# Down weights of a one-token decode block in three loads of 21, 6 and 1 rows in place of five

## The chip, the cores and the metric

The kernel runs on one core of one Trainium2 chip. Its time is the device time of one execution in microseconds. The engines that matter here are TensorE (PE in the profile; its weight loads are PEld), VectorE (DVE), ScalarE (ACT) and SyncE (SP), whose queue issues the loads of weights and caches. The loads themselves are carried by 16 DMA engines.

## The reference

One token passes through a transformer block: layer norm, grouped-query attention over a cache of 65,536 positions, a residual, a second layer norm and a gated feed-forward network. All inputs are bfloat16.

```python
x: [1, 1, 1024]; k_cache, v_cache: [1, 4, 65536, 128]; wq: [1024, 4096]; wo: [4096, 1024]
w_gate, w_up: [1024, 3584]; w_down: [3584, 1024]

def _A_ref(x, k_cache, v_cache, wq, wo):      # 32 query heads on 4 key/value heads
    q = (x @ wq) in heads
    p = softmax(q @ k^T * 128 ** -0.5)
    return (p @ v) joined @ wo

def _B_ref(x, w_gate, w_up, w_down):
    return (gelu(x @ w_gate) * (x @ w_up)) @ w_down

h = x + _A_ref(layernorm(x), ...)
h2 = h + _B_ref(layernorm(h), ...)
```

The caches are 134 MB, the five weight matrices 39 MB; every byte of them is read once.

## The kernel before

All of it goes through one buffer in SBUF, `ring`, of five units of 16,384 bfloat16 columns on 128 partitions. `load` (L167 issues the transfer on SP's queue) places each load at the next free unit. SP issues the loads in the order of the program and waits, before each, until the matmuls that read the old contents of those columns are done, and until the old contents have landed. Transfers are carried out in the order of their issue.

The attention part takes keys and values of four heads through the ring. Then come the output projection (`wo`, two loads), the residual and the second layer norm, and the feed-forward part, in which this change lies. The vector of the token is the stationary operand (32 columns, of which one is used), and the weights stream past it. Four matmuls at a time work side by side, each on 32 columns of the array. The gate matrix `wg` comes in one load of 7168 KB (ring columns 16384 to 45055), the up matrix `wu` in two loads of 3584 KB (columns from 49152 on). Their products are copied out of PSUM, turned by TensorE (`turned`, L156), and joined to the activation `act_bf`, which `padded` writes to `actz`.

The down matrix has 3584 rows; partition p holds 28 of them, one after the other, so "28 rows" here means 28 rows for each of the 128 partitions, 256 KB a row. The loop at the end loads them in groups. `at[0] = 0` and the offset `c0 * D` put all groups side by side at the ring's columns 0 to 28671: a row takes 1024 columns. Columns 0 to 16383 last held the second load of `wo`, columns from 16384 on the first rows of `wg`; a row of `wg` takes 3584 columns. So a group that ends at column 14336 waits for `wo` alone, and one that ends at 21504 or 27648 waits for the matmuls of gate rows 0 and 1, or 0 to 3.

For each row, `out_mm` issues four matmuls of 256 columns that add up in one PSUM tile, `f_ps`, which already holds the residual. After the last row, VectorE copies it to `o_fin` (L558), and SP stores that (L559).

`keep_busy` issues matmuls whose product, `w_ps`, nobody reads: 512 columns each against the identity. They stand in TensorE's queue before the matmuls of the first group, and after those of each group in the number that `busy` gives. TensorE works in the order of its queue. All matmuls go through `mm` (L145 loads the stationary operand first, L147 reuses it).

Of the kernel before, what the change touches and what calls it, by code (L numbers as in the profile page):

```python
# [17 lines left out]
def kernel(  # L18
# [123 lines left out]
    def mm(out, lhsT, rhs, start, stop, loaded=False, tile_position=None, skip_group_check=False):  # L142
        t = nc.tensor
        if not loaded:
            return pe(t.matmul(out, lhsT=lhsT, rhs=rhs, start=start, stop=stop, tile_position=tile_position,  # L145
                               skip_group_check=skip_group_check))
        op = t.add_instruction(mybir.InstMatmult(  # L147
            name=nc.get_next_instruction_name(), engine=t.engine, start_tensor_calc=start, stop_tensor_calc=stop,
            tile_size=(lhsT.shape[0], lhsT.shape[1]), tile_position=tile_position or (0, 0), ldweights=False,
            bass_skip_group_check=skip_group_check,  # L150
            ins=[t.lower_ap(rhs), t.lower_ap(lhsT, for_matmul_weights=True)], outs=[t.lower_ap(out, opt=True)]))
        reuses.add(op.ins.name)
        return pe(op)
# [6 lines left out]
    def load(src, off=0):  # L160
        n, w = src.shape[1], src.shape[2]
        units = -(-(off + n * w) // CW)
        o = at[0] * CW + off
        assert o + n * w <= NBUF * CW
        at[0] = (at[0] + units) % NBUF
        tv = ring[:, o:o + n * w]
        nc.sync.dma_start(out=tv.rearrange("p (n w) -> p n w", w=w), in_=src)  # L167
        return tv.rearrange("p (n w) -> p n w", w=w)
# [348 lines left out]
    for c0 in range(0, DC, GB):  # L517
        wu = load(uv[:, c0:c0 + GB, :])
# [16 lines left out]
        nc.vector.tensor_tensor(out=by_j(act_bf, j0, nj), in0=src, in1=by_j(gl, j0, nj), op=ALU.mult)  # L535

    wd_v = B_w_down.rearrange("(p c) n -> p c n", p=P)
    sizes = [14, 7, 4, 2, 1]
    assert sum(sizes) == FC
    actz = padded(rows, act_bf[:], FC, "actz")  # L540
    w_ps = row_bank("w_ps")
# [1 line left out]
    def keep_busy(n, src):  # L543
        for _ in range(n):
            mm(w_ps[:], ident_bf[:], src, True, True)

    keep_busy(8, wu[:, 0, 0:512])
    busy = [3, 2, 1, 0, 0]
    c0 = 0
    for sz, nb in zip(sizes, busy):  # L550
        at[0] = 0
# [38 lines left out]
```

## Time and profile before

| what | value |
|---|---|
| time, median of 5 executions | 408.49 us (408.39 to 409.21) |
| the profiled execution | 408.59 us, of which the span of instructions 406.8 us |
| bytes read | 173.02 MB, 425 GB/s over the span |
| TensorE busy | 291.3 us, 72% of the span |
| VectorE busy | 202.7 us, 50% |
| down loads, issued at | 357.54, 371.38, 372.24, 372.91 and 373.28 us |
| gate matrix, first matmul | 369.46 us |
| second half of the up matrix, first matmul | 386.36 us |
| last instruction of the result's path | copy at 403.69 us, store issued at 404.13 us |

Times in the profile count from the start of the span. "Busy" of TensorE includes the time in which a matmul drains, so that matmuls overlap each other. PEclk is the share of full speed that TensorE's clock was granted. In the profile, `ring<-in_B_w_down_dram` is a down load, `f_ps<-ring,actz` a matmul of a down row, and `w_ps<-ring,ident_bf` an unread product.

### The profile page before, as it was taken

What the parts mean: (1) busy time and instruction counts of PE and PEld (TensorE: products, weight loads), DVE (VectorE), ACT (ScalarE), POOL (GpSimd) and SP (SyncE); (2) the same over time, 40 slices, a digit from 0 to 9 for tenths busy, and PEclk for the clock granted to TensorE, in tenths of its full rate; (3) what the DMA queues carried; (4) which work ended last, traced back from release to release, by engine and by line L of the source; (5) the groups of instructions that cost most, each with busy time, mean ns of one, the idle gap of its engine ahead of it and who ended that gap; (6) DMA issues with size and microseconds to landing.
All of it is one profiled execution on the core that took longest, in us unless ns stands there. A gap on an engine that the chain in (4) does not pass through costs nothing.

```text
span 406.8 us, 2667 instructions
## 1 busy us (share of the span) xinstructions
PE 291.3 (72%) x1495; PEld 60.6 (15%) x743; DVE 202.7 (50%) x185; ACT 44.7 (11%) x67; POOL 7.4 (2%) x17
## 2 busy tenths in 40 slices
PE   0446767769977699599867958976597969636283
PEld 0111111111111112111111120111111101212041
DVE  1118899954978369146973950879543000220110
ACT  1010000032000040100003220000041000100000
POOL 2000000000000000000000000000100000100000
PEclk9996999887989999799899997999989899886889
DMA  9999999999999999999999999999999999999995
GB/s 374 451 412 458 417 429 451 413 445 424 412 467 419 409 499 414 409 422 422 493 414 416 435 425 435 414 480 412 445 445 419 446 393 445 436 437 423 426 422 222
DMA packets 5212, 173.19 MB, mean 426 GB/s; under 512 B 584, under 2 KB 592, under 8 KB 848
## 3 DMA queue, kind: packets, MB, share of 16 engines
q1 hardware_dynamic: 5192, 173.02, 98.7%
q8 instruction: 9, 0.15, 0.1%
q14 instruction: 3, 0.02, 0.0%
q10 hardware_dynamic: 8, 0.00, 0.0%
HBM read 173.02 MB, written 0.00 MB: 425 GB/s over the span
## 4 chain that ended last, share of the span: by engine, by line
DMA 62%; PE 28%; DVE 7%; ACT 1%; issue 0%; SPq 0%; ACTq 0%
DMA ring<-in_A_v_cache_dram 40%; PE acc_ps L147 12%; DMA ring<-in_A_k_cache_dram 7%; DMA ring<-in_B_w_down_dram 7%; DMA ring<-in_B_w_gate_dram 7%; PE qk_ps L145 6%; PE qk_ps L147 6%; DVE ring L281 5%; PE acc_ps L145 4%; DVE mx L302 2%; ACT sc L301 1%; PE wg_ps L145 0%; PE wg_ps L147 0%; SPq L167 0%; DVE o_fin L558 0%
## 5 line engine op out<-in xcount | busy, mean ns | idle before, releaser
L281 DVE STREAM_TRANSPOSE ring<-ring 128x2048 uint32<-128x2048 uint32 x64 | 142.6, 2280 | 36.9 <-DMA ring<-in_A_k_cache_dram 36.9
L145 PE MATMUL qk_ps<-ring,wsel 128*128 128x512 bf16 x256 | 100.7, 393 | 36.0 <-DVE mx L302 23.6
L147 PE MATMUL acc_ps<-ring,pT 128*128 128x512 bf16 x384 | 113.3, 407 | 0.0
L147 PE MATMUL qk_ps<-ring,wsel 128*128 128x512 bf16 x256 | 100.7, 393 | 0.0
L145 PE MATMUL acc_ps<-ring,pT 128*128 128x512 bf16 x128 | 52.3, 409 | 21.5 <-DMA ring<-in_A_v_cache_dram 21.5
L145 PEld LDWEIGHTS <-wsel 128*128 128x128 bf16 x256 | 25.4, 99 | 135.3 <-issue 134.5
L301 ACT COPY sc<-qk_ps 128x1024 f32<-128x1024 f32 x16 | 16.2, 1010 | 181.4 <-PE qk_ps L147 181.3
L302 DVE TENSOR_REDUCE mx<-qk_ps 128x1 f32<-128x1024 f32 x16 | 19.5, 1222 | 27.4 <-ACT sc L301 27.4
L145 PEld LDWEIGHTS <-pT 128*128 128x128 bf16 x128 | 13.3, 104 | 120.2 <-issue 111.3
L357 DVE COPY acc_sb<-acc_ps 32x512 f32<-32x512 f32 x8 | 5.4, 672 | 36.8 <-PE acc_ps L147 36.7
L330 DVE STREAM_TRANSPOSE pT<-pe_r 128x1024 bf16<-128x1024 bf16 x16 | 19.0, 1226 | 6.2 <-ACT pe_r L327 6.2
L327 ACT ACTIVATE pe_r<-sc,nbias 128x1024 bf16<-128x1024 f32 x16 | 18.2, 1140 | 34.4 <-DVE nbias L322 33.7
L359 ACT COPY acc_sb<-acc_ps 32x512 f32<-32x512 f32 x8 | 4.6, 576 | 65.2 <-DVE acc_sb L357 65.1
L145 PE MATMUL ln_tot<-ln_s,ones_f 128*128 128x1 f32 x8 | 1.9, 312 | 12.0 <-DVE ln_s L199 10.1
L145 PE MATMUL wu_ps<-ring,hnz 128*32 128x512 bf16 x32 | 4.7, 504 | 8.0 <-DMA ring<-in_B_w_up_dram 8.0
L145 PE MATMUL wg_ps<-ring,hnz 128*32 128x512 bf16 x32 | 4.6, 516 | 7.9 <-DMA ring<-in_B_w_gate_dram 7.9
L145 PE MATMUL q_ps<-ring,xnz 128*32 128x512 bf16 x32 | 4.9, 600 | 6.7 <-DMA ring<-in_A_wq_dram 5.1
L145 PE MATMUL o_ps<-sel,acc_sb 128*128 128x8 f32 x32 | 4.2, 257 | 6.5 <-DVE rl L371 5.7
L145 PE MATMUL f_ps<-ring,actz 128*32 128x256 bf16 x112 | 4.0, 274 | 4.8 <-DMA ring<-in_B_w_down_dram 4.8
L315 DVE TENSOR_REDUCE gm<-mxT_ps 1x8 f32<-1x128 f32 x4 | 1.1, 279 | 12.5 <-PE mxT_ps L156 12.5
L237 DVE COPY q_ev<-q_ps 128x512 f32<-128x512 f32 x1 | 0.7, 690 | 12.0 <-PE q_ps L147 12.0
L237 DVE COPY wg_ev<-wg_ps 128x512 f32<-128x512 f32 x1 | 0.7, 693 | 11.6 <-PE wg_ps L145 11.6
(103 smaller groups left out, 88.4 us busy)
## 6 DMA issues: line engine op xcount, KB each, us to landing
ring<-in_A_k_cache_dram SPq DMA_DIRECT2D x16, 4096.0 KB, 34.1
ring<-in_A_wq_dram SPq DMA_DIRECT2D x2, 4096.0 KB, 16.5
ring<-in_A_wo_dram SPq DMA_DIRECT2D x2, 4096.0 KB, 30.9
ring<-in_B_w_gate_dram SPq DMA_DIRECT2D x1, 7168.0 KB
ring<-in_B_w_up_dram SPq DMA_DIRECT2D x2, 3584.0 KB, 30.7
ring<-in_B_w_down_dram SPq DMA_DIRECT2D x1, 3584.0 KB, 37.2
ring<-in_B_w_down_dram SPq DMA_DIRECT2D x1, 1792.0 KB
ring<-in_B_w_down_dram SPq DMA_DIRECT2D x1, 1024.0 KB, 29.2
```

Of the source, the lines that this page charges most:

```text
L145: return pe(t.matmul(out, lhsT=lhsT, rhs=rhs, start=start, stop=stop, tile_position=tile_position, skip_group_check=skip_group_check))
L147: op = t.add_instruction(mybir.InstMatmult(name=nc.get_next_instruction_name(), engine=t.engine, start_tensor_calc=start, stop_tensor_calc ...
L237: nc.vector.tensor_copy(out=dst, in_=src)
L281: dv(nc.vector.transpose(out=kt[:, c * w:(c + 1) * w], in_=kt[:, c * w:(c + 1) * w]))
L301: ac(nc.scalar.copy(out=sc[:], in_=flat))
L302: dv(nc.vector.tensor_reduce(out=state[("mx", g)][:, li:li + 1], in_=flat, axis=AX.X, op=ALU.max))
L315: dv(nc.vector.tensor_reduce(out=gm[:], in_=mxT_ps[:].rearrange("o (x h) -> o h x", h=rep), axis=AX.X, op=ALU.max))
L327: ac(nc.scalar.activation(out=pe_r[:], in_=state.pop(("sc", g, li))[:], func=ACT.Exp, bias=nbias[:, 0:1], scale=scale, accum_out=lpart[:, ...
L330: dv(nc.vector.transpose(out=pT[:].rearrange("p m c -> p (m c)"), in_=pe_r[:]))
L357: dv(nc.vector.tensor_copy(out=acc_sb[sl, :], in_=acc[sl, c, :]))
L359: ac(nc.scalar.copy(out=acc_sb[sl, :], in_=acc[sl, c, :]))
```

## The change

The 28 rows of the down matrix come in three loads of 21, 6 and 1 rows instead of five of 14, 7, 4, 2 and 1. Twenty unread products instead of eight stand before the first group's matmuls; three follow the first group, and none the later ones. In all there are 23 unread products instead of 14. The rows, the order in which they are added, and their places in the ring are the same.

```diff
     wd_v = B_w_down.rearrange("(p c) n -> p c n", p=P)
-    sizes = [14, 7, 4, 2, 1]
+    sizes = [21, 6, 1]
     assert sum(sizes) == FC
     actz = padded(rows, act_bf[:], FC, "actz")
     w_ps = row_bank("w_ps")
 
     def keep_busy(n, src):
         for _ in range(n):
             mm(w_ps[:], ident_bf[:], src, True, True)
 
-    keep_busy(8, wu[:, 0, 0:512])
-    busy = [3, 2, 1, 0, 0]
+    keep_busy(20, wu[:, 0, 0:512])
+    busy = [3, 0, 0]
     c0 = 0
     for sz, nb in zip(sizes, busy):
         at[0] = 0
         wv = load(wd_v[:, c0:c0 + sz, :], c0 * D)
         for cc in range(sz):
             c = c0 + cc
             out_mm(actz[:, c, :], lambda g: wv[:, cc, g * OW:(g + 1) * OW], False, c + 1 == FC)
         c0 += sz
         keep_busy(nb, wv[:, 0, 0:512])
```

## The prediction

> **What bounds the kernel now.** I read the page first, then the chain of waits over the last part, then the timeline of the tail, then sums over chosen stretches for the clock. The page says that the program waits for data almost throughout:
>
> ```profile
> span 406.8 us, 2667 instructions
> DMA 62%; PE 28%; DVE 7%; ACT 1%; issue 0%; SPq 0%; ACTq 0%
> ```
>
> The chain of waits (start, length, what) shows what ends the program: the last down load, issued at 373.28, is in the queue for 30.02 us, and only one row of matmuls, one copy and the store follow it.
>
> ```profile
> 372.91 0.33 SPq L167
> 373.23 0.04 issue
> 373.28 30.02 DMA ring<-in_B_w_down_dram
> 403.30 0.04 issue
> 403.35 0.32 PE f_ps L145 x4
> 403.66 0.03 issue
> 403.69 0.42 DVE o_fin L558
> ```
>
> So the end can move in two ways: the last byte lands at another time, or TensorE is not done with what came before it. The timeline of the tail (start, length, engine, what) shows how much room TensorE has. x56 is 14 rows of four matmuls, x28 is 7 rows; w_ps are the unread products; the brackets hold TensorE's idle time before.
>
> ```profile
> 391.38 1.89 PE L145 MATMUL w_ps<-ring,ident_bf 128*128 128x512 bf16 x8
> 394.82 1.71 PE L145 MATMUL f_ps<-ring,actz 128*32 128x256 bf16 x56 [1.56 <-DMA ring<-in_B_w_down_dram]
> 396.47 0.82 PE L145 MATMUL w_ps<-ring,ident_bf 128*128 128x512 bf16 x3
> 399.06 0.95 PE L145 MATMUL f_ps<-ring,actz 128*32 128x256 bf16 x28 [1.77 <-DMA ring<-in_B_w_down_dram]
> 401.50 0.62 PE L145 MATMUL f_ps<-ring,actz 128*32 128x256 bf16 x16 [0.95 <-DMA ring<-in_B_w_down_dram]
> 402.72 0.40 PE L145 MATMUL f_ps<-ring,actz 128*32 128x256 bf16 x8 [0.28 <-DMA ring<-in_B_w_down_dram]
> 403.35 0.29 PE L145 MATMUL f_ps<-ring,actz 128*32 128x256 bf16 x4 [0.22 <-DMA ring<-in_B_w_down_dram]
> ```
>
> Rows 14, 21, 25, 27 and 28 are thus usable at 394.82, 399.06, 401.50, 402.72 and 403.35; no gap between matmul groups exceeds 1.77 us. From these rows: 14 rows and the step to the products take 1.65 us, 7 rows 0.88, so a row at full clock costs (1.65 - 0.88) / 7 = 0.11 us, with some 0.1 us more for the step to a product. A product costs (1.89 - 0.38) / 7 = 0.216 us, 0.38 being the length of a single one.
>
> **The clock.** In sums over stretches (us, PE busy, ..., PEclk, DMA share, GB/s) the granted clock is 1.00 or 0.50, and it changes only at multiples of 3.41 us from one another: 382.79, 389.62 and 406.69 among others. Cut at those steps, the rows show what decides the next stretch:
>
> ```profile
> 85.83:89.25 3.42, 1.35 (x8) 0.47 (x4) 0.65 (x3) 1.07 (x2) 0.00 (x0) 1.00 1.02 441
> 89.25:92.66 3.41, 1.81 (x5) 0.25 (x2) 3.02 (x3) 3.23 (x7) 0.00 (x0) 0.50 0.96 413
> 328.18:331.59 3.41, 1.48 (x7) 0.19 (x2) 0.00 (x0) 0.00 (x0) 0.00 (x0) 1.00 0.89 384
> 331.59:335.01 3.42, 1.95 (x10) 0.20 (x2) 0.00 (x0) 0.00 (x0) 0.00 (x0) 1.00 1.07 460
> 167.75:171.17 3.42, 2.62 (x7) 0.26 (x2) 0.00 (x0) 0.00 (x0) 0.00 (x0) 0.50 1.04 450
> 171.17:174.58 3.41, 3.41 (x10) 0.30 (x2) 0.00 (x0) 0.00 (x0) 0.00 (x0) 0.50 1.04 452
> 396.45:399.86 3.41, 1.64 (x35) 0.97 (x31) 0.00 (x0) 0.00 (x0) 0.00 (x0) 1.00 0.96 407
> 399.06:399.86 0.80, 0.80 (x28) 0.66 (x27) 0.00 (x0) 0.00 (x0) 0.00 (x0) 1.00 1.00 420
> ```
>
> A stretch with 1.35 us of matmuls is followed by half clock; one with 1.48 us is not. At half clock, 2.62 us of work does not bring the clock back (the stretch from 171.17 is still at 0.50); a full one does. The tail of before holds 1.64 us in the stretch to 399.86 and keeps its clock, but by little.
>
> **The change, part by part.**
>
> *Issues.* Five loads are issued at 357.54, 371.38, 372.24, 372.91 and 373.28. The new first load ends at ring column 21504, where the old second one ended, so it waits for the same gate matmuls (row 1) and goes out at about 371.38, 13.84 us later than the old first load. The second ends at column 27648, as the old fourth did: about 372.91; the third follows 0.33 later. Behind them on SP's queue stands only the store of the result. What hides the delay is the up matrix: its second half becomes usable at 386.36, so the queue still has 15.0 us of transfers when the first down load joins it. I take 0; without that cover it would be up to 13.84. Two issues of 0.33 disappear from an idle SP: 0.
>
> *Transfer.* The bytes and their order stay. From the usable times, a row took 0.604 us in the load of 14 (386.36 to 394.82), 0.606 in that of 7, 0.61 in those of 4 and 2, 0.625 in the last. All 28 rows at 0.604 would end 0.07 earlier; six rows at 0.625 instead of 0.61 would end 0.09 later. The trace has no load of 21 rows; the nearest, 14 and 7, differ by 0.002 a row, so I take 0 and keep -0.07 and +0.09.
>
> *Products.* Twelve more, at 0.216, end at 391.38 + 0.38 + 19 x 0.216 = 395.86 instead of 393.27, in time in which TensorE waited anyway: 0 by themselves. The first load is usable only at 399.06, though, so TensorE now stands idle for 3.20 us, where it stood for at most 1.77.
>
> *Matmuls at full clock.* 84 from 399.06 take 21 x 0.11 + 0.1 = 2.4, to 401.5; three products and the step out of them 0.75, to 402.2. The second load is usable at 402.72, so 0.5 us is left over, and that is all the cover there is. Then 6 rows x 0.11 = 0.66: the last row starts at 403.38 instead of 403.35, +0.03. At full clock the change is worth nothing: +0.03, with ends -0.07 and +0.12.
>
> *Matmuls at the clock that is granted.* With the steps of the profiled execution, the stretch from 396.45 to 399.86 holds only the first 0.80 us of the new matmuls (last row above), below the 1.35 that lost the clock. So at 399.86 it falls to half. By then 7 rows are done. The up matmuls show the price of half clock: a group of 512 columns every 0.43 us against 0.216, so a down row costs 0.213 (256 columns). 14 rows x 0.213 = 2.98, to 402.84; the step to the products, 0.1; products at 0.43 until 403.27, where a full stretch brings the clock back with 2.2 of them to go: 0.48, to 403.75; 6 rows, 0.66, to 404.41. The last row starts 1.06 later than in before. Counting the fraction of a row under way at 399.86 gives 0.95; I take 1.0. The 0.5 us of cover is inside this sum. Copy and store follow unchanged.
>
> *Sum.* The profiled execution took 408.59 us, a span of 406.8 and 1.8 around it, 0.10 above the median 408.49. 408.59 + 1.0 = 409.6 for its kind, 409.5 for the median.
>
> *How often the clock falls.* Nothing says that the steps stand at the same place in every execution. If the products end at 395.86, a step between 397.9 and 399.06 closes a stretch with under 1.4 us of products, and one between 399.06 and 400.5 closes one with under 1.4 us of rows: 2.6 of 3.41 us, three quarters of all places. But in some of those places the clock comes back late after the up matmuls, because the stretch that should bring it back holds the idle 0.5 us before the transposes (about 2.95 us of work, between the 2.62 that failed and the 3.09 that sufficed in the stretch before 372.55). Then the twenty products run at 0.43, end near 397 to 399, and close the gap themselves. That leaves between a quarter and three quarters; I take a little over half.
>
> The Trainium skill bears on this in "TensorE: Matmul & The Clock Gate". Its last table (Why this matters for your kernels) says that gaps of more than about 3 us between bursts drop the clock to half; its section on the clock gate says that it takes an idle window of about 3.4 us. By the first, every execution would lose the clock here and the sum would be +1.0; by the second, a gap of 3.2 never fills a window and the sum would be +0.03. The row with 1.35 us of work agrees with neither word for word: little work is enough, idleness isn't needed.
>
> **Rivals.**
> 1. *The clock stays up in most executions*: same time, 408.5, between 408.35 and 408.75. For it: products at half clock fill the gap, and a step between 395.9 and 397.9 does no harm. Against it: the profiled execution's own steps.
> 2. *Faster*: two loads fewer end the stream earlier. It decides only if each removed load were worth 0.41 us, 0.82 together; the rows show 0.07 in all. 407.7 if so.
> 3. *The clock falls before 399.06 and isn't back*: 21 x 0.213 + 0.1 + 3 x 0.43 + 6 x 0.213 puts the last row at 406.2, about +3: 411.5. It needs a step between 397.9 and 398.9 and a next stretch too thin. Possible in a single execution, unlikely as a median.
> 4. *The first load comes too late for the queue*, its lead of 15.0 us notwithstanding: each us of empty queue costs one. Against it: the last load of before, issued at the same moment, ran without a gap.
> 5. *The change doesn't do what it says*: twenty products do not reach the first load in the profiled execution (3.20 us short). This is part of the forecast, not against it.
>
> **How the numbers follow.** A measurement of this kernel can tell about 0.2%, 0.82 us, from no change. The clock falls in most executions: 0.52, at 409.5, with its own range 409.2 to 409.8; of this, 0.07 stays within 0.82. Rival 1: 0.38. Rival 2: 0.04. Rivals 3 and 4: 0.06. Slower 0.52 - 0.07 + 0.06 = 0.51; same 0.38 + 0.07 = 0.45; faster 0.04. The range spans the first two cases, 408.35 to 409.8, and leaves out a tenth.
>
> **What the profile after would show.** PE idle of about 3.2 us before an x84 group of f_ps at 399.1; PEclk 0.50 somewhere between 398 and 403; that group lasting 3.3 to 4.3 us instead of 2.4; no DMA wait before the last row, the chain ending through a long PE piece instead of one of 0.32; DMA share still 1.0 around 386. I am wrong if PEclk stays 1.00 there (then the time is rival 1's), if the products last to 398, or if the last load lands at another time than 403.3.

## The result, and the profile after

The changed kernel takes 409.50 us (median of 26 executions, 408.47 to 410.3) against 408.56 us for the kernel before (46 executions, 408.35 to 409.21). The medians differ by 0.94 us, 0.23%; the ratio of the means is 1.0017 with a 95% interval of 1.0012 to 1.0023. It is slower, by about what was forecast. Among all kernels of this study, three single executions took 28 to 357 us longer than the rest of their kernel; the comparisons leave them out.

The 26 executions form two groups with nothing between 409.06 and 409.43: ten from 408.47 to 409.06, mean 408.69, and sixteen from 409.43 to 410.3, mean 409.69. The mean, and with it the ratio, lies between the groups; the median lies in the slower one, because that group has more than half of the executions. The profiled execution, 409.78 us, is of the slower group.

The page of the changed kernel:

```profile
span 407.8 us, 2682 instructions
DMA 61%; PE 29%; DVE 7%; ACT 1%; issue 0%; SPq 0%; ACTq 0%
```

The shares are almost those of before; the difference is in the tail. The end of its chain of waits (start, length, what):

```profile
371.12 27.61 DMA ring<-in_B_w_down_dram
398.74 0.04 issue
398.78 4.01 PE f_ps L145 x84
402.80 0.84 PE w_ps L145 x3
403.63 0.91 PE f_ps L145 x28
404.54 0.02 issue
404.56 0.42 DVE o_fin L558
```

In before, the last load ended the chain with 0.32 us of matmuls behind it. Now it is the first down load that is on the chain, and 5.76 us of uninterrupted TensorE work follows it. The landing of the second and third loads no longer shows: TensorE was not ready for them (the third, issued at 373.0, landed 30.0 us later, at 403.0, while the last seven rows began at 403.63).

The timeline of the same tail (the bracket holds TensorE's idle time before):

```profile
391.12 4.48 PE L145 MATMUL w_ps<-ring,ident_bf 128*128 128x512 bf16 x20
398.78 4.01 PE L145 MATMUL f_ps<-ring,actz 128*32 128x256 bf16 x84 [3.18 <-DMA ring<-in_B_w_down_dram]
402.73 0.90 PE L145 MATMUL w_ps<-ring,ident_bf 128*128 128x512 bf16 x3
403.56 0.95 PE L145 MATMUL f_ps<-ring,actz 128*32 128x256 bf16 x28
```

And the sums over stretches cut at the steps of the clock (us, PE busy, PEld, DVE, ACT, POOL, PEclk, DMA share, GB/s):

```profile
392.69:396.10 3.41, 2.91 (x14) 1.21 (x13) 0.00 (x0) 0.00 (x0) 0.00 (x0) 1.00 0.93 404
396.10:399.52 3.42, 0.74 (x28) 0.74 (x31) 0.00 (x0) 0.00 (x0) 0.00 (x0) 1.00 0.94 404
399.52:402.93 3.41, 3.41 (x65) 2.74 (x58) 0.00 (x0) 0.00 (x0) 0.00 (x0) 0.50 0.60 246
402.93:406.34 3.41, 1.58 (x31) 0.75 (x29) 0.42 (x1) 0.00 (x0) 0.00 (x0) 1.00 0.02 5
```

The stretch that holds the gap has 0.74 us of matmuls, and the next one runs at half clock. It is full, so the clock is back at 402.93, in time for the last seven rows. In before, the same place held 1.64 us.

### The profile page after: what moved, and what is told of

The parts are those of the page before. It is cut to its first block, busy times and chain, and to the rows that moved or that the text cites. A ratio compares the mean times of both kernels' runs of the same rounds, so it can differ in the third digit from the quotient of the medians.

```text
span 407.8 us, 2682 instructions
## 1 busy us (share of the span) xinstructions
PE 294.9 (72%) x1504; PEld 63.4 (16%) x752; DVE 202.7 (50%) x185; ACT 44.7 (11%) x67; POOL 7.4 (2%) x17
## 4 chain that ended last, share of the span: by engine, by line
DMA 61%; PE 29%; DVE 7%; ACT 1%; issue 0%; SPq 0%; ACTq 0%
DMA ring<-in_A_v_cache_dram 40%; PE acc_ps L147 12%; DMA ring<-in_A_k_cache_dram 7%; DMA ring<-in_B_w_gate_dram 7%; DMA ring<-in_B_w_down_dram 7%; PE qk_ps L145 6%; PE qk_ps L147 6%; DVE ring L281 5%; PE acc_ps L145 4%; DVE mx L302 2%; ACT sc L301 1%; PE f_ps L145 1%; PE wg_ps L145 0%; PE wg_ps L147 0%; PE w_ps L145 0%
## 5 line engine op out<-in xcount | busy, mean ns | idle before, releaser
L145 PE MATMUL f_ps<-ring,actz 128*32 128x256 bf16 x112 | 5.0, 350 | 3.2 <-DMA ring<-in_B_w_down_dram 3.2
```

## Experiments

The theory: the time is lost because TensorE has too little work in some 3.41 us stretch before the first load is usable, so its clock falls to half for the 21 rows that follow. The main rival: the grouping itself costs, since more rows wait for one landing. The edits are to the changed kernel unless it is said otherwise. Each ratio is to the kernel before, run beside the variant (median 408.57 or 408.56 us), with its 95% interval.

**Twenty-eight products**

```diff
-    keep_busy(20, wu[:, 0, 0:512])
+    keep_busy(28, wu[:, 0, 0:512])
```

> Theory (the granted clock falls because TensorE has too little work before the first load): 28 products in place of 20 end 8 x 0.216 = 1.7 us later, at about 397.3 in the count of before, and leave a gap of 1.5 us instead of 3.2, as wide as those of before. No 3.41 us stretch is then thin enough, the clock stays up, and the time is 408.6 (408.45 to 408.8) with no execution above 409.2. Rival (the grouping itself costs, since 21 rows of matmuls wait for one landing): nothing changes, median 409.5, executions spread over 408.5 to 410.3.

Measured: 408.72 us, ratio 1.0003 (0.9994 to 1.0012); all ten executions from 408.45 to 409.0. The slower group is gone, with the loads as they are in the change. The timeline of its profiled execution shows the gap and the 84 matmuls:

```profile
399.18 2.48 PE L145 MATMUL f_ps<-ring,actz 128*32 128x256 bf16 x84 [1.46 <-DMA ring<-in_B_w_down_dram]
402.82 0.95 PE L145 MATMUL f_ps<-ring,actz 128*32 128x256 bf16 x28 [0.41 <-DMA ring<-in_B_w_down_dram]
```

The 21 rows take 2.48 us instead of 4.01, and TensorE waits 0.41 us for the second load, as the forecast had it for full clock. Its stretches:

```profile
397.01:400.42 3.41, 1.95 (x52) 1.43 (x53) 0.00 (x0) 0.00 (x0) 0.00 (x0) 1.00 0.83 355
400.42:403.83 3.41, 2.78 (x78) 1.95 (x67) 0.02 (x1) 0.00 (x0) 0.00 (x0) 1.00 0.45 179
```

With 1.95 us in the stretch of the gap, the clock stays up. The grouping alone, without the lost clock, costs nothing that can be measured, so it is ruled out as the cause of the loss.

**Eight products, as before, with the three loads**

```diff
-    keep_busy(20, wu[:, 0, 0:512])
+    keep_busy(8, wu[:, 0, 0:512])
```

> The three loads with the eight products of before: the gap before the first load is 5.8 us. Theory: some 3.41 us stretch holds next to nothing wherever the steps stand, so every execution loses the clock; where it is lost early and the next stretch is thin, it is lost for longer. Median 410.0 (409.5 to 410.6), lowest above 409.2. Rival (grouping itself): as with 20, median 409.5 with a part of the executions at 408.6.

Measured: 410.40 us, ratio 1.0040 (1.0028 to 1.0052); five executions, 409.76 to 410.72. None is as fast as before, as the theory had it; the median is above the 410.0 that it named. The profiled execution is the fastest of the five. Its stretches show that the clock fell earlier than in the change and came back earlier:

```profile
395.17:398.58 3.41, 0.00 (x0) 0.00 (x0) 0.00 (x0) 0.00 (x0) 0.00 (x0) 1.00 0.94 404
398.58:401.99 3.41, 2.97 (x59) 2.49 (x61) 0.00 (x0) 0.00 (x0) 0.00 (x0) 0.50 0.88 371
401.99:405.41 3.42, 2.41 (x62) 1.52 (x55) 0.42 (x1) 0.00 (x0) 0.00 (x0) 1.00 0.13 46
```

By the medians, the loads of the change without its products cost 1.83 us, about twice as much as the change. Why the other four executions took 0.1 to 1.0 us longer than this one was not seen in a profile.

**Twenty products with the five loads of before** (edit of the kernel before)

```diff
-    keep_busy(8, wu[:, 0, 0:512])
+    keep_busy(20, wu[:, 0, 0:512])
```

> The five loads of before with twenty products and 3, 2, 1 after: the products end at 395.9, 1.0 us after the first load is usable, and its 14 rows start late by that, but TensorE has 1.8 us to spare before the second. Theory: no long gap, no loss, 408.55 (408.4 to 408.7). Rival (the twelve more products cost by themselves, through the power or the queue of TensorE): 409.5.

Measured: 408.37 us, ratio 0.9994 (0.9986 to 1.0003); 408.07 to 408.61. The products cost nothing by themselves. Their end at 395.6 delays the first 14 rows, and that is made up before the second load, for which TensorE still waits:

```profile
398.87 0.95 PE L145 MATMUL f_ps<-ring,actz 128*32 128x256 bf16 x28 [0.79 <-DMA ring<-in_B_w_down_dram]
```

**No products after the first load**

```diff
-    busy = [3, 0, 0]
+    busy = [0, 0, 0]
```

> Twenty products before the first load, none after it. Theory: where the clock has fallen, the three products are on the path (0.84 us in the chain of the changed kernel), and without them the slow executions lose 0.6 to 0.8 us; the fast ones stay. Median 408.8 (408.6 to 409.0), highest 409.5. Rival (the three products keep the clock up for the second load): without them the clock falls more often or for longer, median 409.5 or above.

Measured: 408.90 us, ratio 1.0006 (0.9997 to 1.0015); eleven executions from 408.48 to 409.55. The median is 0.6 us below that of the change, as the theory had it, and the rival's 409.5 or above did not come. One execution is above 409.4. The three products, meant to fill a wait, lie on the path when the clock has fallen: 0.84 us in the chain above. The profiled execution, 409.08 us, had full clock throughout the tail, so the case of a fallen clock without the three products was not seen in a profile, and the times alone do not tell which of the other ten lost the clock.

This profile shows something else. The gap before the first load is as long as in the change, and yet the clock stays up:

```profile
399.11 2.48 PE L145 MATMUL f_ps<-ring,actz 128*32 128x256 bf16 x84 [3.11 <-DMA ring<-in_B_w_down_dram]
```

```profile
394.17:397.59 3.42, 1.83 (x9) 0.72 (x8) 0.00 (x0) 0.00 (x0) 0.00 (x0) 1.00 0.85 366
397.59:401.00 3.41, 1.89 (x72) 1.89 (x75) 0.00 (x0) 0.00 (x0) 0.00 (x0) 1.00 0.89 377
```

Here a step, at 397.59, stands inside the gap, so that the stretch before it still holds 1.83 us of products and the one after it 1.89 us of rows. With the same twenty products, the place of the steps decides.

**Twenty-four products**

```diff
-    keep_busy(20, wu[:, 0, 0:512])
+    keep_busy(24, wu[:, 0, 0:512])
```

> 24 products end at 396.7 in the count of before, 2.3 us ahead of the first load. Theory, by counting the places of the steps in which a 3.41 us stretch holds under 1.4 us of work: half of the places instead of three quarters, and, scaled by the 16 of 26 slow executions that 20 products gave, about 4 in 10 executions slow, at 409.4 to 409.9, the others at 408.6. Median 408.6 to 408.9. Rival (a gap as such, above some 3 us, loses the clock): no execution slow, all within 408.4 to 409.0.

Measured: 408.63 us median; eight executions from 408.34 to 408.88 and four from 409.86 to 410.08; ratio 1.0011 (1.0002 to 1.0021). The profiled execution is one of the four, 410.08 us:

```profile
399.25 4.14 PE L145 MATMUL f_ps<-ring,actz 128*32 128x256 bf16 x84 [2.36 <-DMA ring<-in_B_w_down_dram]
```

```profile
396.34:399.75 3.41, 1.05 (x23) 0.64 (x25) 0.00 (x0) 0.00 (x0) 0.00 (x0) 1.00 0.89 380
399.75:403.16 3.41, 3.41 (x75) 2.96 (x64) 0.00 (x0) 0.00 (x0) 0.00 (x0) 0.50 0.66 272
```

A gap of 2.36 us was enough to lose the clock, since the stretch around it held 1.05 us of work. That rules out the rival of a gap above some 3 us. The share of executions above 409.2 us, 4 of 12, is near the 4 in 10 expected, though twelve executions fix it only roughly; their times are a little above the 409.4 to 409.9 that was expected.

**Forty products**

```diff
-    keep_busy(20, wu[:, 0, 0:512])
+    keep_busy(40, wu[:, 0, 0:512])
```

> 40 products at full clock end at 391.4 + 0.38 + 39 x 0.216 = 400.2, 1.1 us after the first load is usable; 21 rows 2.4, three products 0.75, six rows 0.66 put the last row at 404.0, 0.65 later than before. Where the clock comes back late after the up matmuls, the products run at half clock for longer and the end moves by 2 to 3 us. Theory: 409.3 to 411.5, median about 409.8. Rival (more products are always safer): 408.6.

Measured: 409.36 us, ratio 1.0019 (1.0011 to 1.0028); 409.02 to 410.0. Too many products cost, as expected, but less than the median of 409.8 that was expected: 0.80 us, near the 0.65 of the plain overrun. No execution shows the 2 to 3 us of products at half clock. In the profiled execution the clock was up from 389.08 on.

**Fuller gaps with the five loads, and the twenty products once more** (edits of the kernel before)

```diff
-    keep_busy(8, wu[:, 0, 0:512])
-    busy = [3, 2, 1, 0, 0]
+    keep_busy(14, wu[:, 0, 0:512])
+    busy = [6, 4, 2, 0, 0]
```

> The five loads of before with 14 products and 6, 4, 2 after, so that no gap before a group exceeds 1.2 us. Theory: the upper end of before's own times (408.8 to 409.2 in a quarter of its executions) comes from a clock that falls in the gaps of up to 1.8 us in a few places of the steps; with the gaps filled, 408.4 (408.2 to 408.6), highest under 408.8. Rival (that scatter is the loads'): as before, 408.55 with single ones at 408.9 to 409.2.

> The five loads of before with twenty products again, which gave 408.37 against 408.57. Theory as for the fuller gaps: 408.4, highest under 408.8, a ratio of 0.9995. Rival (chance): 408.55, ratio 1.000.

Measured: 408.49 us, ratio 0.9998 (0.9989 to 1.0007), and 408.60 us, ratio 0.9999 (0.9990 to 1.0008). The repeat did not confirm the 408.37 of the first run, and one execution of the fuller kernel stands at 408.99. These two runs gave no support to the theory that lost clock makes the upper end of before's times; where that scatter of up to 0.9 us comes from stays open. No kernel of this study is measurably faster than the one before.

| first load, unread products ahead of it | gap in the profiled execution | executions above 409.2 us | median |
|---|---|---|---|
| 14 rows, 8 (before) | 1.56 us | 1 of 46 | 408.56 |
| 21 rows, 8 | 5.31 us | 5 of 5 | 410.40 |
| 21 rows, 20 (the change) | 3.18 us | 16 of 26 | 409.50 |
| 21 rows, 24 | 2.36 us | 4 of 12 | 408.63 |
| 21 rows, 28 | 1.46 us | 0 of 10 | 408.72 |
| 21 rows, 40 | none | 7 of 11 | 409.36 |

The loss is smallest in between: with too few products the clock falls, with too many they delay the rows.

## Why the prediction was right, and where it fell short

*Issues and transfer.* As forecast, the first load goes out at 371.12, when the second up half still needs 14.98 us until its first matmul at 386.10. From there to the landing of 21 rows it is 12.68 us, and 12.70 in before (386.36 to 399.06). A later issue and a longer load cost nothing; rivals 2 and 4 found nothing to stand on. The last load landed at 403.0 where 403.3 was forecast; the second up half, too, came 0.26 us earlier here.

*Products and gap.* Forecast 3.20 us of idle time, measured 3.18.

*Clock.* Forecast: 0.80 us of matmuls in the stretch, a fall to half, and a return after one full stretch. The rows above show 0.74, 0.50 and 1.00. That the steps stood almost where they stood in the profile of before was chance. At half clock, 65 matmuls in 3.41 us make 0.21 us a row, as in the sum. The 84 matmuls took 4.01 us, inside the 3.3 to 4.3 that were named.

*Sum.* From the first matmul of the second up half to the end of the last row it is 18.44 us (386.10 to 404.54) against 17.30 (386.36 to 403.66) in before: 1.14 more, where the sum had 1.06 with whole rows and 0.95 with fractions. The two groups of executions lie 1.00 apart in their means. That the median of 409.50 meets the forecast of 409.5 to the hundredth is luck: it is a time at the lower end of the slower group, whose mean is 409.69, and it would lie in the faster group had four more of the 26 kept their clock.

*How often.* The bounds were a quarter and three quarters, and 0.52 was taken; 16 of 26 is 0.62. The lower bound rested on a clock that comes back late because the stretch after the up matmuls holds the idle 0.5 us. The profiles speak against that: such a stretch held 3.04 us of work with eight products (388.34 to 391.75) and 3.04 without the three (387.35 to 390.76), and full clock followed both times; 2.93 and 2.95 us in the stretches that hold the start of the up matmuls (24 and 40 products) also sufficed. So three quarters is what is left, an estimate with 1.4 us as the line, and 26 executions do not tell it from 0.62. Rival 3, a clock that is not back for the last rows, was put at 411.5; no execution is above 410.3.

That the places of the steps differ from execution to execution is shown by the profiles: a step stands 0.74 us after the start of the first down row in the change, 0.50 after it with 24 products, 1.24 after it with 28, 0.44 before it with eight and 1.52 before it without the three. No run set the place of a step, so the cause of one execution's group is inferred, except in those that were profiled. One more sign for it: with 24 products the granted clock, averaged over the whole execution, was 0.916 to 0.921 in the four above 409.2 us and 0.881 to 0.908 in the eight others. One lost stretch in the tail would lower this average by 0.004 (half of 3.41 us in 408), so the four differ from the rest long before the tail. In the change the two groups overlap in it (0.879 to 0.920 and 0.899 to 0.912).

*What fell short.* The chances treated the median as if it lay in one case or the other. A mixture was no case of its own: 0.62 x 1.00, with the faster group 0.09 above the mean of before, moves the mean by 0.70 us, 0.17%, under the 0.82 us that the chance of slower was defined by, while the median moves by 0.94, over it. The step that gave only 0.07 of the lost clock to "within 0.82" was too confident by that. The expectation for forty products carried over the clock that comes back late, which no profile shows. And the reading that a stretch with 1.35 us of matmuls loses the clock while one with 1.48 us keeps it holds for the rows that were shown, but it is no rule in busy time: the trace of before also has a stretch with 1.92 us that was followed by half clock (last section). Within the tails, too, stretches with 1.53 to 1.64 us went either way. The forecast did not hang on this: its stretch was put at 0.80 us.

*The page weighed against the rows.* The Trainium skill, "TensorE: Matmul & The Clock Gate", gives about 3 us of gap in its last table (Why this matters for your kernels) and an idle window of about 3.4 us in its section on the clock gate. Neither limit held here: a gap of 2.36 us lost the clock with 24 products and one of 3.18 us with 20, while one of 3.11 us, without the three products, kept it. The work in the stretch decided, as in the rows of before.

## What to carry to other kernels

Before a load is made larger, look at what TensorE does until it lands: the bytes came at the same rate here, but the gap took the clock from the matmuls that followed. Judge such a gap by the work left in a 3.41 us stretch placed at its worst around it, and look for two groups in the times of single executions; a median over a few of them can show either. Unread matmuls that fill a wait are free only as long as the wait is there: the three behind the first load were on the path in the profiled executions that had lost the clock.

## What the runs showed of the hardware

In all ten profiles the granted clock of TensorE was 1.00 or 0.50 and changed only at steps that lie a multiple of 3.41 us apart; where the steps stood differed from one profiled execution to another. In the tails of the kernels with three loads, the stretches that held the gap before the first load lost the clock with 0.00, 0.74 and 1.05 us of matmuls and kept it with 1.83 us and more. So a stretch that is a third full can lose the clock, and a gap of 2.36 us was enough. In the whole traces at half clock, no stretch with 2.62 us of work or less brought it back, and every one with 2.77 us or more did.

Busy time alone draws no sharp line at full clock. In the tails, 1.58 us (the last row shown of the change) and 1.64 us (before, 396.45 to 399.86) kept it, while 1.53 us (without the three products, 401.00 to 404.41) and 1.64 us (the second run of twenty products with the five loads, 400.65 to 404.07) were followed by half clock. At the end of the attention part of before, this still fuller stretch (same columns as above) lost it:

```profile
348.66:352.07 3.41, 1.92 (x15) 1.59 (x15) 0.91 (x5) 1.05 (x2) 1.12 (x2) 1.00 1.13 490
352.07:355.49 3.42, 3.16 (x32) 0.77 (x20) 0.20 (x1) 0.00 (x0) 0.88 (x2) 0.50 1.01 436
```

Its fifteen matmuls have 8 to 128 columns, those of the tail from the unread products on 256 or 512. Short matmuls may count for less, since busy time includes the time in which a matmul drains; no run tested that.
